# Two loads reordered, the constants' transfer moved behind them, and one test of the first group moved from ScalarE to VectorE

## The chip, the core and the metric

The kernel runs on one core of a Trainium2 chip. A core has five engines that run side by side, each through its own instructions in order: TensorE (PE; its weight loads are PEld), VectorE (DVE), ScalarE (ACT), GpSimd (POOL) and SyncE (SP, which here only issues DMAs; SPq and ACTq are the queues that issue). Transfers run on 16 DMA engines. The metric is the device time of one execution in microseconds, as the median of several runs.

## The reference

A gated linear attention with a complex gate, then a feed-forward block:

```python
mag = np.sqrt(a_re * a_re + a_im * a_im)
scale = np.minimum(mag, 0.999) / (mag + 1e-06)
a_re_n, a_im_n = (a_re * scale, a_im * scale)
for t in range(S):
    new_re = ar * S_re - ai * S_im
    new_im = ar * S_im + ai * S_re
    S_re, S_im = (new_re + kv, new_im)
    y[:, :, t] = einsum('bhd,bhde->bhe', q[:, :, t], S_re)
# x: (B*S, H*D)
h = x @ w_in
solu = h * softmax(h)
ln = (solu - mean) / sqrt(var + 1e-06) * g_ln
return ln @ w_out
```

B = 4, H = 8, S = 768, D = 48; 3072 tokens of width 384 go through a hidden width of 1024. The weights arrive as float64.

## The kernel before

The sequence is cut into six stretches of 128 positions. Two batches of one stretch form a **group** (12 groups, numbered 0 to 11); a tile of a group is 128 positions by 768 columns (2 batches x 8 heads x 48). Each group holds two **chunks**, 24 in all, which go through attention and the feed-forward block one after the other.

For a group, `prep_steps` turns the gate into a logarithm of its size and an angle, so that the recurrence becomes running sums, which TensorE makes by a triangular matrix out of a table of constants `mats`. The steps, with their lines:

- `inverse` (L824, L825, ScalarE): lr = Ln(ar), x0 = Exp(-lr), which is 1/ar.
- `ratio` (L830, L831, VectorE): ai = ai * x0, x0 = ar * x0. The second is 1 up to the error of the inverse.
- `sure` (L834, ScalarE): the test of the inverse. It adds up (x0 - 1) squared over the row into `seen`; a verdict at the end of the kernel compares this with a bound, and a general version follows if it is exceeded.
- `tangent` (L839, VectorE): x0 = (x0 - 2) * ai, a corrected ratio, written over x0.
- `square`, `secant` (L842, L845, ScalarE): ar = x0 squared, u = Ln(ar + 1). `fourth` (L848, ScalarE): ar squared into ai, with its sum into `seen`, another test.
- `size` (L852, VectorE), `eps` (L855, L856, ScalarE), `lnm` (L859, VectorE): the logarithm of the clamped size, in lr.
- `total` (L881, TensorE): running sums of lr; `grow` (L893) and `decay` (L896, ScalarE): their exponentials into ai and ar, with which k and q are scaled (L908, L904, VectorE).
- `angle` (L922, ScalarE): the arctangent of x0, in place; then phases, `nearest` (L938, into the tile f), sine and cosine.

For group 0 alone, the steps from `inverse` to `angle` and the loads of a_re and a_im are done in two halves of 384 columns, a and b. The test `sure` of half b adds up in a slot of its own. For the other groups both halves are one instruction.

The order of the instructions on all engines is written out by hand in the string `ORDER`: a list of step names with the number of their group, chunk or weight piece. Each engine receives its instructions in this order, and waits at each for what it needs. All loads are issued by SP in this order, so a DMA that has to wait keeps those behind it waiting. Ahead of the first step stand a load of ScalarE's table, the DMA of the constants, issued by ScalarE (L1280), and some memsets.

The weights are fetched in seven pieces (`fetch`), of which ScalarE (`raised`, L752) and VectorE (`convert`, L758 to L762) make float32 values in between the first groups. `last` (L900) sends the last row of the decays through a DMA.

Tiles named ar and ai have two buffers each, by turns for the groups; lr, x0 and u have one, f has one.

Of the kernel before, what the change touches and what calls it, by code (L numbers as in the profile page):

```python
# [516 lines left out]
init:0 load_aia:0 load_ara:0 inversea:0 load_arb:0 ratioa:0 load_aib:0 surea:0 load_q:0 tangenta:0 fetch:5 fetch:1  # L517
inverseb:0 squarea:0 ratiob:0 secanta:0 sureb:0 sizea:0 load_v:0 tangentb:0 epsa:0 load_k:0 lnma:0 squareb:0 secantb:0
fourthb:0 sizeb:0 total0:0 epsb:0 fourtha:0 raised:5 lnmb:0 decay0:0 grow0:0 total1:0 grow1:0 decay1:0 fetch:0 trig:0
anglea:0 convert:5 phase0:0 last:0 raised:1 qs0:0 angleb:0 convert:1 phase1:0 nearest0:0 part0:0 turn_ends:0  # L520
nearest1:0 ks0:0 ks1:0 sina:0 cosa:0 load_ai:1 qs1:0 part1:0 q2:0 tot:0 sinb:0 k2:0 cosb:0 exp:0 qt1:0 load_ar:1 qT1:0
raised:0 q2:1 kt1:0 k2:1 convert:0 kT1:0 inverse:1 ratio:1 kt0:0 qt0:0 qT0:0 kT0:0 fetch:2 score1:0 fetch:6 qt0:1
qT0:1 load_vr:0 score0:0 qt1:1 sure:1 raised:2 load_q:1 mask0:0 values:0 tangent:1 kt1:1 fetch:3 square:1 secant:1
turned_x:0 convert:2 qT1:1 up0:0 fetch:4 raised:6 size:1 eps:1 convert:6 lnm:1 fourth:1 onward:0 up1:0 gain:0 total1:1
load_k:1 kT1:1 raised:3 exp0:0 grow1:1 total0:1 decay0:1 grow0:1 carry:1 convert:3 solu0:0 decay1:1 trig:1 angle:1
kt0:1 phase1:1 ks1:1 qs0:1 kT0:1 add:1 phase0:1 ks0:1 score1:1 raised:4 nearest0:1 score0:1 nearest1:1 convert:4
part0:1 carry:0 part1:1 mean:0 mean:3 mean:7 add:0 sin:1 cos:1 mask0:1 load_q:2 q2:2 k2:2 mean:1 zt0:0 exp:1 load_ar:2
mean:4 mean:2 inverse:2 values:1 mean:5 kqb:2 turned_x:1 load_ai:2 ratio:2 mean:6 zT0:0 meansum:0 again:5 last:1
centre:3 centre:7 up1:1 sure:2 tangent:2 load_v:1 kqt0:2 square:2 zt1:0 centre:1 centre:2 secant:2 centre:0 centre:4
size:2 centre:6 eps:2 centre:5 up0:1 k2:3 turn_ends:1 qs1:1 score1:2 lnm:2 onward:1 centred:0 load_vr:1 score0:2 tot:1  # L530
down0:0 total0:2 zT1:0 total1:2 load_k:2 q2:3 exp0:1 fourth:2 mask0:2 down1:0 solu0:1 decay0:2 grow0:2 grow1:2
load_ar:3 decay1:2 kqb:3 trig:2 mixed:1 zt0:1 kqt0:3 last:2 values:2 angle:2 spread:0 zT0:1 on:2 phase1:2 ks1:2 norm:0
qs0:2 turned_x:2 phase0:2 carry:2 load_ai:3 nearest1:2 nearest0:2 up0:2 part1:2 part0:2 sin:2 add:2 cos:2 ks0:2 k2:4
q2:4 centred:1 exp:2 zt1:1 zT1:1 inverse:3 scale:0 up1:2 kqb:4 score1:3 score0:3 down0:1 mask0:3 ratio:3 exp0:2
turn_ends:2 spread:1 sure:3 solu0:2 load_q:3 values:3 tangent:3 load_v:2 down1:1 square:3 tot:2 turned_x:3 secant:3
size:3 load_k:3 carry:3 qs1:2 up0:3 kqt0:4 eps:3 norm:1 up1:3 k2:5 onward:2 zt1:2 lnm:3 lh:3 zt0:2 exp0:3 q2:5 scale:1
zT0:2 zT1:2 fourth:3 score1:4 ll:3 score0:4 mixed:0 total0:3 load_vr:2 total1:3 down0:2 kqb:5 down1:2 solu0:3 decay0:3
grow0:3 grow1:3 decay1:3 mask0:4 add:3 centred:2 trig:3 blocks:3 values:4 angle:3 on:3 xh:3 kqt0:5 store:1 store:0
spread:2 xl:3 last:3 phase1:3 turned_x:4 phase0:3 ks0:3 ks1:3 qs0:3 nearest0:3 score1:5 load_ar:4 centred:3 score0:5
nearest1:3 carry:4 load_ai:4 norm:2 part0:3 up0:4 part1:3 sin:3 cos:3 up1:4 mask0:5 turn_ends:3 exp:3 add:4 scale:2  # L540
k2:6 q2:6 away:3 inverse:4 values:5 exp0:4 kqb:6 ratio:4 down0:3 load_q:4 solu0:4 spread:3 turned_x:5 sure:4 load_v:3
tangent:4 qs1:3 down1:3 carry:5 kqt0:6 square:4 blocks:4 secant:4 size:4 onward:3 up0:5 away:4 eps:4 k2:7 norm:3 up1:5
q2:7 lnm:4 lh:4 tot:3 fourth:4 score1:6 ll:4 score0:6 exp0:5 total0:4 load_vr:3 load_k:4 kqb:7 total1:4 kqt0:7 solu0:5
scale:3 decay0:4 grow0:4 grow1:4 decay1:4 mask0:6 add:5 down0:4 trig:4 down1:4 centred:5 values:6 angle:4 on:4 xh:4
centred:4 qs0:4 xl:4 spread:4 last:4 store:2 phase1:4 turned_x:6 phase0:4 ks1:4 nearest0:4 ks0:4 nearest1:4 blocks:5
score1:7 carry:6 load_ai:5 part0:4 load_ar:5 part1:4 norm:4 score0:7 up0:6 sin:4 add:6 turn_ends:4 cos:4 exp:4 scale:4
away:5 store:3 inverse:5 mask0:7 up1:6 k2:8 q2:8 kqb:8 values:7 spread:5 exp0:6 ratio:5 down0:5 sure:5 load_q:5
solu0:6 turned_x:7 load_v:4 tangent:5 down1:5 square:5 qs1:4 kqt0:8 blocks:6 secant:5 onward:4 carry:7 up0:7 norm:5
size:5 eps:5 q2:9 k2:9 away:6 load_vr:4 lnm:5 up1:7 load_k:5 lh:5 fourth:5 scale:5 exp0:7 score1:8 ll:5 score0:8
total0:5 tot:4 kqb:9 total1:5 down0:6 kqt0:9 solu0:7 grow1:5 decay1:5 mask0:8 decay0:5 grow0:5 trig:5 down1:6 add:7  # L550
centred:7 blocks:7 values:8 angle:5 on:5 inspect:5 xh:5 centred:6 xl:5 spread:6 phase1:5 last:5 qs0:5 store:4
turned_x:8 phase0:5 ks1:5 load_ar:6 nearest1:5 nearest0:5 ks0:5 carry:8 load_ai:6 score0:9 score1:9 part1:5 part0:5
mask0:9 up1:8 sin:5 norm:6 up0:8 cos:5 add:8 turn_ends:5 scale:6 exp:5 inverse:6 store:5 k2:10 q2:10 values:9 kqb:10
ratio:6 exp0:8 solu0:8 away:7 turned_x:9 onward:5 down0:7 load_q:6 sure:6 down1:7 load_v:5 spread:7 tangent:6 square:6
blocks:8 qs1:5 kqt0:10 carry:9 secant:6 fourth:6 up0:9 norm:7 size:6 k2:11 away:8 eps:6 lnm:6 tot:5 load_vr:5 up1:9
q2:11 lh:6 scale:7 exp0:9 load_k:6 score0:10 score1:10 ll:6 total0:6 kqb:11 total1:6 down0:8 kqt0:11 solu0:9 grow1:6
decay1:6 mask0:10 decay0:6 grow0:6 trig:6 down1:8 add:9 centred:9 blocks:9 angle:6 values:10 on:6 xh:6 centred:8
store:6 xl:6 qs0:6 spread:8 last:6 phase1:6 turned_x:10 phase0:6 nearest0:6 ks1:6 nearest1:6 score1:11 carry:10
load_ai:7 score0:11 ks0:6 load_ar:7 away:9 part0:6 part1:6 cos:6 up0:10 sin:6 norm:8 mask0:11 up1:10 turn_ends:6
scale:8 exp:6 add:10 inverse:7 spread:9 store:7 values:11 k2:12 q2:12 kqb:12 ratio:7 exp0:10 down0:9 onward:6 solu0:10  # L560
load_q:7 turned_x:11 sure:7 down1:9 tangent:7 qs1:6 carry:11 load_v:6 kqt0:12 square:7 blocks:10 up0:11 secant:7
size:7 norm:9 eps:7 k2:13 away:10 load_vr:6 scale:9 lnm:7 tot:6 up1:11 q2:13 lh:7 fourth:7 exp0:11 score1:12 load_k:7
ll:7 score0:12 total0:7 kqb:13 total1:7 down0:10 centred:10 kqt0:13 solu0:11 grow1:7 decay1:7 mask0:12 decay0:7
grow0:7 trig:7 down1:10 add:11 blocks:11 angle:7 values:12 on:7 xh:7 last:7 store:8 spread:10 centred:11 qs0:7 xl:7
ks0:7 phase1:7 turned_x:12 phase0:7 nearest1:7 ks1:7 nearest0:7 score0:13 score1:13 part1:7 part0:7 mask0:13 sin:7
load_ar:8 away:11 carry:12 load_ai:8 up0:12 cos:7 add:12 norm:10 turn_ends:7 scale:10 exp:7 store:9 up1:12 k2:14 q2:14
inverse:8 values:13 kqb:14 ratio:8 exp0:12 solu0:12 down0:11 load_q:8 turned_x:13 sure:8 down1:11 load_v:7 tangent:8
carry:13 qs1:7 spread:11 kqt0:14 square:8 blocks:12 secant:8 norm:11 size:8 onward:7 k2:15 tot:7 eps:8 away:12 lnm:8
load_vr:7 fourth:8 up0:13 lh:8 load_k:8 up1:13 q2:15 score1:14 score0:14 ll:8 scale:11 total0:8 kqb:15 total1:8
exp0:13 decay0:8 grow0:8 centred:12 mask0:14 grow1:8 decay1:8 down0:12 kqt0:15 solu0:13 trig:8 down1:12 add:13  # L570
centred:13 blocks:13 angle:8 values:14 on:8 xh:8 store:10 spread:12 xl:8 last:8 phase1:8 turned_x:14 phase0:8 ks0:8
score0:15 qs0:8 nearest0:8 score1:15 ks1:8 nearest1:8 part0:8 carry:14 load_ai:9 part1:8 sin:8 norm:12 mask0:15 cos:8
add:14 load_ar:9 up1:14 turn_ends:8 exp:8 up0:14 away:13 k2:16 q2:16 scale:12 inverse:9 store:11 values:15 kqb:16
ratio:9 exp0:14 spread:13 load_v:8 solu0:14 turned_x:15 sure:9 down0:13 load_q:9 down1:13 tangent:9 blocks:14 square:9
# [38 lines left out]
def whole(ctx, tc, flag, q, k, v, a_re, a_im, moe_w_in, moe_w_out, moe_g_ln, out):  # L613
# [193 lines left out]

    def prep_steps(g):
        ti, b0 = g * GB // B, g * GB % B
        split = g >= 3  # L810

        class Tiles(dict):
            def __missing__(self, nm):
# [27 lines left out]
        def square(cs):  # L841
            nc.scalar.activation(out=st["ar"][:, cs], in_=st["x0"][:, cs], func=AF.Square)  # L842
# [531 lines left out]
```

## Time and profile before

| | us |
|---|---|
| median of 3 runs | 415.65 (415.19 to 415.83) |
| the profiled execution: its time | 415.1 |
| the profiled execution: its span | 413.1 |

| engine | busy us | share of the span |
|---|---|---|
| PE | 379.1 | 92% |
| DVE | 337.0 | 82% |
| ACT | 299.0 | 72% |
| POOL | 64.5 | 16% |

The span lies between the first and the last instruction; the profiled execution's time is 2.0 us longer than its span. The page cuts the span into 40 slices of 10.3 us; a digit is the busy share of a slice in tenths:

```
PE   0368779999999999999999999999999999999995
DVE  3798999779799899899988899889988988855530
ACT  4997977977887777887877976877976967721332
PEclk9999999999999999999999999999999999999998
```

In the first slices TensorE is little used; later on it is full nearly to the end. PEclk is the clock that TensorE was granted. In a row of the order of time, the first number is the start in us from the beginning of the span, the second the duration; then come the engine, the line, the operation, the tile written and the tiles read, and in brackets how long the engine sat idle before and what it waited for.

### The profile page before, as it was taken

To read this page: it belongs to the slowest core of one execution; us is meant where nothing else is said; L and a number is where in the kernel's file an instruction comes from. 1 tells how busy PE (TensorE), PEld (TensorE's weight loads), DVE (VectorE), ACT (ScalarE), POOL (GpSimd) and SP (SyncE) were. 2 spreads that over 40 slices of the span, in tenths; PEclk is the share of its full clock that TensorE was granted. 3 is DMA by queue.
4 is the path that set the end of the run, shared out by engine and by line. 5 is a ranking of instruction groups with operands and counts; after the bars stand their busy time and mean duration, and the time that the engine had idled before them with its cause. 6 is when DMAs were issued, how large, how long until landed. Compare 5 with 4: busy or idle time off the path is not lost.

```text
span 413.1 us, 15874 instructions
## 1 busy us (share of the span) xinstructions
PE 379.1 (92%) x6968; PEld 202.7 (49%) x6968; DVE 337.0 (82%) x414; ACT 299.0 (72%) x487; POOL 64.5 (16%) x140
## 2 busy tenths in 40 slices
PE   0368779999999999999999999999999999999995
PEld 0025334455645554654554554555645656546543
DVE  3798999779799899898899889988988988855530
ACT  4997977977887777887877976877976967721332
POOL 3000000112112112112122112112112122101111
PEclk9999999999999999999999999999999999999998
DMA  9995947695877778877787877967759768797551
GB/s 216 286 280 153 222 101 171 159 211 128 207 165 170 167 177 180 182 157 167 179 175 165 207 163 160 206 157 172 163 138 215 158 155 206 232 208 187 171 216 49
DMA packets 167741, 74.17 MB, mean 180 GB/s; under 512 B 142576, under 2 KB 156016, under 8 KB 166896
## 3 DMA queue, kind: packets, MB, share of 16 engines
q1 hardware_dynamic: 167376, 72.64, 74.7%
q8 instruction: 57, 0.93, 0.9%
q10 hardware_dynamic: 288, 0.43, 0.4%
q14 instruction: 20, 0.16, 0.1%
HBM read 38.87 MB, written 4.72 MB: 106 GB/s over the span
## 4 chain that ended last, share of the span: by engine, by line
PE 81%; ACT 8%; DVE 5%; DMA 2%; issue 1%; SPq 1%; DVEq 0%; ACTq 0%
PE f_h L1128 28%; PE f_o L1193 27%; PE f_y L1087 9%; PE f_score L1054 7%; PE f_d L1095 3%; PE f_L L876 2%; PE f_phase L876 2%; DMA f_q<-in_q_dram 1%; DMA f_ar<-in_a_re_dram 1%; ACT f_cs L951 1%; PE f_y L1203 1%; PE f_o L1203 1%; ACT L986 1%; ACT L989 1%; DVE f_kb L1009 1%
## 5 line engine op out<-in xcount | busy, mean ns | idle before, releaser
L1128 PE MATMUL f_h<-f_w_in,f_xT 128*32 128x512 f32 x1152 | 131.4, 593 | 1.4 <-ACT f_xT L1121 1.2
L1193 PE MATMUL f_o<-f_w_mix,f_zT 128*32 128x384 f32 x1280 | 108.6, 487 | 0.0
L1128 PEld LDWEIGHTS f_h<-f_w_in,f_xT 128*32 128x32 f32 x1152 | 40.9, 110 | 66.4 <-issue 64.3
L1193 PEld LDWEIGHTS f_o<-f_w_mix,f_zT 128*32 128x32 f32 x1280 | 42.8, 110 | 54.1 <-issue 51.5
L1009 DVE STREAM_TRANSPOSE f_kb<-f_kq 128x1536 f32<-128x1536 f32 x22 | 56.5, 2570 | 1.4 <-DMA f_kqT<-f_kb 0.7
L1140 DVE SCALAR_TENSOR_TENSOR f_z<-f_h,f_z 128x1024 f32<-128x1024 f32 x24 | 29.1, 1213 | 13.5 <-ACT f_z L1136 13.5
L1180 POOL TENSOR_SCALAR f_s<-f_s,f_sum 128x1 f32<-128x1 f32 x24 | 11.7, 485 | 182.1 <-ACT f_z L1174 181.9
L1136 ACT ACTIVATE f_z<-f_h 128x1024 f32<-128x1024 f32 x24 | 24.4, 1018 | 21.0 <-PE f_h L1128 21.0
L1087 PE MATMUL f_y<-f_att,f_v 128*16 128x128 f32 (+1 forms) x384 | 36.7, 273 | 0.8 <-DVE f_att L1059 0.8
L1054 PEld LDWEIGHTS f_score<-f_kqT 96*32 96x32 f32 x1536 | 32.5, 112 | 10.0 <-issue 10.0
L1087 PE MATMUL f_y<-f_att,f_vr 128*32 128x128 f32 x384 | 36.8, 273 | 0.0
L1059 DVE TENSOR_TENSOR f_att<-f_score,f_mats 128x1024 f32<-128x1024 f32 x24 | 29.3, 1220 | 8.5 <-PE f_score L1054 8.4
L1054 PE MATMUL f_score<-f_kqT 96*32 96x64 f32 (+3 forms) x1536 | 34.0, 238 | 0.0
L1087 PE MATMUL f_y<-f_kqT,f_state 96*32 96x128 f32 (+1 forms) x640 | 33.2, 272 | 0.0
L1174 ACT ACTIVATE f_z<-f_z,f_less 128x1024 f32<-128x1024 f32 x24 | 27.3, 1138 | 0.0
L869 POOL TENSOR_TENSOR f_ll<-f_lr,f_lh 128x768 fp32r<-128x768 f32 x9 | 16.6, 1849 | 65.6 <-ACT f_lh L864 57.9
L1087 PEld LDWEIGHTS f_y<-f_att,f_v 128*32 128x32 f32 (+1 forms) x384 | 22.0, 103 | 7.5 <-issue 6.4
L1158 DVE STREAM_TRANSPOSE f_zb<-f_z 128x1024 f32<-128x1024 f32 x20 | 24.8, 1238 | 0.0
L1000 DVE TENSOR_TENSOR f_kq<-f_cs,f_k 128x768 f32<-128x768 f32 x24 | 22.9, 955 | 2.1 <-ACT f_cs L951 1.2
L1000 DVE TENSOR_TENSOR f_kq<-f_cs,f_q 128x768 f32<-128x768 f32 x24 | 22.9, 953 | 1.1 <-PE f_d L1095 0.5
L1087 PEld LDWEIGHTS f_y<-f_att,f_vr 128*32 128x32 f32 x384 | 22.3, 109 | 1.7 <-issue 1.7
L1171 POOL TENSOR_SCALAR f_less<-f_sum 128x1 f32<-128x1 f32 x24 | 6.3, 266 | 88.7 <-DVE f_z L1140 88.7
(124 smaller groups left out, 643.9 us busy)
## 6 DMA issues: line engine op xcount, KB each, us to landing
f_kqT<-f_kb SPq DMA_DIRECT2D x88, 192.0 KB, 3.3
f_zT<-f_zb SPq DMA_DIRECT2D x80, 128.0 KB, 3.1
f_raw<-in_moe_w_out_dram SPq DMA_DIRECT2D x14, 384.0 KB, 5.0
f_raw<-in_moe_w_in_dram SPq DMA_DIRECT2D x5, 1024.0 KB, 6.7
f_q<-in_q_dram SPq DMA_DIRECT2D x12, 384.0 KB, 4.9
f_v<-in_v_dram SPq DMA_DIRECT2D x12, 384.0 KB, 5.2
f_k<-in_k_dram SPq DMA_DIRECT2D x12, 384.0 KB, 3.9
out_dram<-f_ot SPq DMA_DIRECT2D x23, 192.0 KB, 3.6
```

Source lines behind the costliest of these rows:

```text
L869: nc.gpsimd.tensor_tensor(out=t, in0=st[src], in1=st[hi].bitcast(FP), op=OP.subtract)
L1000: nc.vector.tensor_tensor(out=t, in0=T["cs", g][:, i * H:(i + 1) * H], in1=heads(T[nm, g][:, i]).unsqueeze(2).to_broadcast([P, H, 2, D]), ...
L1009: nc.vector.transpose(out=t, in_=T["kq", c].rearrange("p n h (f j) -> p j (n h) f", j=3))
L1054: nc.tensor.matmul(out=scores[r0:r0 + 32, x, r:], lhsT=QK[:, r // 32, x], rhs=QK[:, r // 32:, H + x], start=True, stop=True)
L1059: nc.vector.tensor_tensor(out=st["att"].rearrange("p (i u) t -> p i u t", u=2), in0=scores.rearrange("p (i u) t -> p i u t", u=2), in1=mat ...
L1087: nc.tensor.matmul(**product)
L1128: nc.tensor.matmul(out=st["h"][r:r + 32, half * 512:(half + 1) * 512], lhsT=st["xT"][:, c * P + r:c * P + r + 32], rhs=w_in[:, c, half * 5 ...
L1136: nc.scalar.activation(out=z, in_=h, func=AF.Exp, accum_out=sums[:, n:n + 1])
L1140: nc.vector.scalar_tensor_tensor(out=st["z"], in0=st["h"], scalar=1.0, in1=st["z"], op0=OP.mult, op1=OP.mult, accum_out=st["sum"][:, 0:1])
L1158: nc.vector.transpose(out=st["zb"], in_=st["z"].rearrange("p (c s f) -> p s c f", s=4, f=32))
L1174: nc.scalar.activation(out=st["z"], in_=st["z"], func=AF.Square, bias=st["less"], accum_out=st["sum"][:, 1:2])
L1193: nc.tensor.matmul(out=st["o"][rows], lhsT=zT, rhs=w[:, c], start=(c == 0), stop=(c == KF - 1))
```

## The change

It has three parts, all at the start of the kernel; the order behind the first 33 entries of `ORDER` is the same.

- The DMA of the constants leaves its place ahead of all steps on ScalarE's queue and becomes a step of its own on SP's queue, behind the four half loads of a_re and a_im and ahead of q. The first half of a_re is loaded ahead of the first half of a_im.
- For group 0 the test `sure` is done by two VectorE instructions, x0 = x0 - 1 and then x0 * x0 with a sum, in place of one of ScalarE. It stands behind `tangent`.
- So that the test still finds x0, `tangent` of group 0 writes to ai instead; `square` and `angle` read it there, `fourth` writes to f, and `grow` to lr, where the scaling of k reads it.

The order, cut to what differs:

```diff
-init:0 load_aia:0 load_ara:0 inversea:0 load_arb:0 ratioa:0 load_aib:0 surea:0 load_q:0 tangenta:0 fetch:5 fetch:1
-inverseb:0 squarea:0 ratiob:0 secanta:0 sureb:0 sizea:0 load_v:0 tangentb:0 epsa:0 load_k:0 lnma:0 squareb:0 secantb:0
+init:0 load_ara:0 load_aia:0 inversea:0 load_arb:0 ratioa:0 load_aib:0 constants:0 load_q:0 tangenta:0 surea:0 fetch:5
+fetch:1 inverseb:0 squarea:0 ratiob:0 secanta:0 sizea:0 load_v:0 tangentb:0 sureb:0 epsa:0 load_k:0 lnma:0 squareb:0
+secantb:0
...
```

The steps:

```diff
+        tan, up = ("ai", "lr") if g == 0 else ("x0", "ai")
...
         def sure(cs, o=g):
-            nc.scalar.activation(out=st["u"][:, cs], in_=st["x0"][:, cs], func=AF.Square, bias=mone,
-                                 accum_out=seen[:, 1, o:o + 1])
+            x0 = st["x0"][:, cs]
+            if g == 0:
+                nc.vector.tensor_scalar(out=x0, in0=x0, scalar1=-1.0, scalar2=None, op0=OP.add)
+                nc.vector.scalar_tensor_tensor(out=x0, in0=x0, scalar=1.0, in1=x0, op0=OP.mult, op1=OP.mult,
+                                               accum_out=seen[:, 1, o:o + 1])
+            else:
+                nc.scalar.activation(out=st["u"][:, cs], in_=x0, func=AF.Square, bias=mone, accum_out=seen[:, 1, o:o + 1])
 
         def tangent(cs):
             ai, x0 = st["ai"][:, cs], st["x0"][:, cs]
-            nc.vector.scalar_tensor_tensor(out=x0, in0=x0, scalar=2.0, in1=ai, op0=OP.subtract, op1=OP.mult)
+            nc.vector.scalar_tensor_tensor(out=st[tan][:, cs], in0=x0, scalar=2.0, in1=ai, op0=OP.subtract, op1=OP.mult)
 
         def square(cs):
-            nc.scalar.activation(out=st["ar"][:, cs], in_=st["x0"][:, cs], func=AF.Square)
+            nc.scalar.activation(out=st["ar"][:, cs], in_=st[tan][:, cs], func=AF.Square)
...
         def fourth(cs, o=g):
-            nc.scalar.activation(out=st["ai"][:, cs], in_=st["ar"][:, cs], func=AF.Square, accum_out=seen[:, 0, o:o + 1])
+            nc.scalar.activation(out=st["f" if g == 0 else "ai"][:, cs], in_=st["ar"][:, cs], func=AF.Square,
+                                 accum_out=seen[:, 0, o:o + 1])
...
         def grow(i):
-            nc.scalar.activation(out=st["ai"][:, i * DM:(i + 1) * DM], in_=st["L", i], func=AF.Exp, scale=-1.0)
+            nc.scalar.activation(out=st[up][:, i * DM:(i + 1) * DM], in_=st["L", i], func=AF.Exp, scale=-1.0)
...
-            nc.vector.scalar_tensor_tensor(out=x, in0=st["ai"][:, i * DM:(i + 1) * DM], scalar=MOST_K, in1=x, op0=OP.min,
+            nc.vector.scalar_tensor_tensor(out=x, in0=st[up][:, i * DM:(i + 1) * DM], scalar=MOST_K, in1=x, op0=OP.min,
...
         def angle(cs):
-            nc.scalar.activation(out=st["x0"][:, cs], in_=st["x0"][:, cs], func=AF.Arctan)
+            nc.scalar.activation(out=st["x0"][:, cs], in_=st[tan][:, cs], func=AF.Arctan)
```

The constants:

```diff
     to_exp()
-    nc.scalar.dma_start(out=mats, in_=nc.inline_tensor(fast_constants(), name="f_mats_np").ap().rearrange("p (n t) -> p n t", n=5))
...
+    def constants():
+        nc.sync.dma_start(out=mats, in_=nc.inline_tensor(fast_constants(), name="f_mats_np").ap().rearrange("p (n t) -> p n t", n=5))
+
+    steps["gain", 0], steps["constants", 0] = gain, constants
```

## The prediction

> **What bounds the kernel now.** I read the span in slices first, then busy time by stretch, then the order of time in the first 20 us. The answer by stretch has, for each engine, busy microseconds and (instructions):
>
> ```profile
> core 0: us, PE busy (x) PEld busy (x) DVE busy (x) ACT busy (x) POOL busy (x), PEclk, DMA share, GB/s
> 0.00:10.00 10.00, 0.00 (x0) 0.00 (x0) 3.36 (x14) 4.39 (x9) 3.48 (x11) 1.00 0.89 210
> 10.00:20.00 10.00, 3.01 (x16) 0.40 (x16) 7.02 (x13) 9.45 (x20) 0.00 (x0) 1.00 0.99 301
> 20.00:30.00 10.00, 6.25 (x34) 2.51 (x34) 9.32 (x13) 9.21 (x16) 0.00 (x0) 1.00 0.98 273
> ...
> 100.00:200.00 100.00, 99.84 (x1942) 54.30 (x1930) 89.26 (x104) 79.31 (x128) 17.71 (x36) 1.00 0.77 172
> ```
>
> From about 60 us on TensorE is full (99.84 of 100 us) at a granted clock of 1.00, so nothing in the change touches its rate; but it can't fill until the first group has been prepared. From 10 to 60 us ScalarE and VectorE run at 9 of 10 us and hand work to each other. The change acts ahead of that. What it can do is start the dense stretch earlier; then everything behind moves as a block. The order of time shows the head (start, duration, engine, line, idle before):
>
> ```profile
> 0.72 0.45 SPq L706 DMA_DIRECT2D f_ai<-in_a_im_dram  x1
> 0.75 0.39 ACTq L1280 DMA_DIRECT2D f_mats<-f_mats_np  x1
> ...
> 1.23 2.38 SPq L706 DMA_DIRECT2D f_ar<-in_a_re_dram  x2
> ...
> 5.58 0.52 ACT L824 ACTIVATE f_lr<-f_ar 128x384 f32<-128x384 f32 x1 [3.58 <-DMA f_ar<-in_a_re_dram]
> 6.13 0.52 ACT L825 ACTIVATE f_x<-f_lr 128x384 f32<-128x384 f32 x1
> 6.69 0.56 DVE L830 TENSOR_TENSOR f_ai<-f_ai,f_x 128x384 f32<-128x384 f32 x1 [4.34 <-ACT f_x L825]
> 7.28 0.56 DVE L831 TENSOR_TENSOR f_x<-f_ar,f_x 128x384 f32<-128x384 f32 x1
> ...
> 7.87 0.61 ACT L834 ACTIVATE f_u<-f_x,f_bias 128x384 f32<-128x384 f32 x1 [1.22 <-DVE f_x L831]
> ...
> 8.39 0.19 ACT L834 ACTIVATION_READ_ACCUMULATOR f_u<-f_x,f_bias 128x1 f32 x1
> 8.49 0.51 ACT L824 ACTIVATE f_lr<-f_ar 128x384 f32<-128x384 f32 x1
> 8.61 0.56 DVE L839 SCALAR_TENSOR_TENSOR f_x<-f_x,f_ai 128x384 f32<-128x384 f32 x1 [0.78 <-ACT f_u L834]
> ...
> 15.61 0.56 DVE L859 SCALAR_TENSOR_TENSOR f_lr<-f_lr,f_u 128x384 f32<-128x384 f32 x1 [1.33 <-ACT f_u L856]
> ```
>
> The first computation waits 3.58 us for a_re, which is issued behind a_im. Then the test (L834) holds up two things: the tangent (L839), which overwrites what it reads, and the second half's inverse (8.49), queued behind it on ScalarE although its a_re landed at 6.46. The last line, lnm of the second half at 15.61, opens the dense stretch. Its new start is the number to find.
>
> **a_re first, constants behind.** Landings before, from issue plus time to landing: a_im first half 4.6, a_re first half 5.56, a_re second 6.46, a_im second 7.36. The DMA answers in 0.2 us windows, by queue (packets, MB, share of 16 engines), from 2.6 and from 3.4 us:
>
> ```profile
> q10 hardware_dynamic: 25, 0.06, 79.7%
> q1 hardware_dynamic: 13, 0.00, 6.0%
> ...
> q1 hardware_dynamic: 272, 0.05, 127.5%
> ```
>
> q10 is the constants, q1 the loads. The loads' first packet comes at about 2.62, 1.90 after issue, and until 3.1 they go packet for packet against the far larger ones of the constants. Then 272 per 0.2 us: a half's 1024 packets take 0.75 us. Counting them up, the first load's last packet is at 3.84; it landed 0.78 later.
>
> Now a_re is issued at 0.72 with nothing beside it. Latest: it lands when the first load did, 4.62. Middle: same first packet, full rate at once, 2.65 + 0.75 + 0.78 = 4.18. Nearest row: a_im of the second group, same 192-byte runs, issued at 20.00 into idle engines, starts at 21.22 and, with its ramp, has 1024 packets through 2.19 after issue; that gives 0.72 + 2.19 + 0.78 = 3.69. The constants' own first packet came 0.95 after issue, as a weight fetch's at 38.79 did, so nothing points to a slow start-up. I take 3.85, close to that row, keeping a third of the gap to the middle case. Gain at the first Ln: 5.58 - 3.85 = **1.73** (bounds 0.96 to 1.89). a_im's first half follows at about 4.7, the next halves at 5.55 and 6.4, by 0.75 to 0.85 each.
>
> Here the Trainium skill speaks against the move: "DMA: Bandwidth & Descriptors", Rules for kernel authors, says that queues of different engines share the same 16 DMA engines and interleave, so that the issuing queue only decides who pays the issue time. By that alone the constants' move saves nothing and costs SP 0.39; the swap of order alone would stay: 0.96. But the packet counts show that interleaving is what delays the first load. I go by them.
>
> **What the queues pay.** SP issues the constants (0.39) ahead of q, fetch 5, fetch 1, v, k and fetch 0. The constants' packets take 1.13 us of 16 engines (q10's shares summed); about 0.4 of that fell where loads can now run, so everything behind them lands some 0.7 later. Cover, with users 2.1 earlier (below): fetch 5 lands 11.6, now 12.3, first used (ScalarE, L752) at 15.99, now 13.9; q 9.2, used at 18.65; fetch 1 15.06, used by VectorE at 19.12; k 18.1, used at 23.22; fetch 0 20.9, used at 28.51. The tightest has 1.2 us left. Constants: behind four halves, last packet about 6.6, landed 7.5; the first matmul wants them at about 11.2. SP is free of fetch 0 at about 17.0 and its next step, the end rows, is ready at 16.6: 0.4 late, against 1.5 of slack before TensorE reads them at 23.48. No cost.
>
> **The test on VectorE.** Per half ScalarE loses L834 with its read of the accumulator, 0.71 on the path. VectorE gains a subtraction and an accumulating product behind the tangent. Subtraction: L758 took 552 ns for 768 and 686 for 1024 columns, so about 0.35 for 384 (0.56 if it ran like a TENSOR_TENSOR). Product: 0.55 like L852; its accumulator read is 0.08 at L1140 and overlaps. With gaps 0.03, 0.96 a half: more than on ScalarE, but nothing needs its result. The trace has no accumulating product of two SBUF operands (L1140 reads PSUM). For it the skill's "Vector Engine (DVE) Microarchitecture Reference", section 7, states half throughput with two non-bf16 SBUF sources, as none is left to read the accumulator. L852 without accumulation ran 384 columns in 0.55; halved, some 0.95. I take 0.55, the nearest row; the rule's 0.40 more lies on the path once.
>
> **The sum, in order of time.** ScalarE inverse a 3.85 to 4.92 (two of 0.52). VectorE ratio a 4.96 to 6.11, tangent a to 6.70, test a to 7.66. ScalarE meanwhile does inverse b from 5.55 to 6.62 (before: 8.49), then square a 6.73, secant a to 7.87. VectorE ratio b follows the test, 7.65 to 8.80, then size a 8.72 to 9.27. Here ScalarE waits: VectorE has become the later one. Eps a 9.29 to 10.54; tangent b (9.19) and test b (to 10.71) lie under that, lnm a 10.63. ScalarE square b 10.44, secant b to 11.59, fourth b to 12.10; size b 11.62 to 12.17; eps b 12.19 to 13.45; lnm b at **13.48** instead of 15.61: 2.13 earlier, 1.73 from the landing and 0.40 from the test. ScalarE's 1.42 us of tests do not become 1.42 us of gain, since test a now stands in front of ratio b and size a.
>
> **Edits at nothing.** Tangent, grow and fourth go to other tiles. fourth's tile f is next written by nearest on the same engine; grow's lr is read last by the k scaling at 24.2 and next written by the second group's inverse at 30.03: 5.8 us of cover, without which that Ln would wait. The second group's a_im has its own buffer.
>
> **Behind lnm b.** ScalarE and VectorE are back to back to 60 us, and their feeds have slack. The odd-head values land at about 33.9 for a product at 36.05; the DMA idle time at 20.3 to 21.3 closes up, so they move about 0.8 and have 0.9 left, and ScalarE picks that product up only at 38.61. So I carry 2.1 whole to the end: span 413.1 to 411.0, that run 415.1 to 413.0; from the median of 415.65, **413.55**.
>
> **Rivals.**
> First, my forecast, 60%: 413.55, own range 413.2 to 414.3 (first landing at 3.69, or at 4.62).
> Second, the dearer test: half throughput and a slow subtraction, 0.40 + 0.21 on the path: gain 1.5, 414.15. For it: the skill's statement and no near row. Against: L852. 12%.
> Third, the transfers hold the head back. The DMA share is 0.98 from 10 to 30 us, and the bulk gets later, not earlier. If a fetch of 20 to 35 us binds, only the closed-up idle time of 0.8 is won: 414.85. Against: the slacks above. 16%.
> Fourth, slower: SP stalls on the constants. One load there (k) took 6.24 us to issue[...]. If the fifth issue met that, fetch 5 would land at 11.6 + 6.2 = 17.8 instead of in time for 15.99, and ScalarE holds decay and grow behind it: 1.8 slower, 417.45. It decides from a stall of 4.4 us on. Against: only some 0.4 MB stands ahead of the constants, and the second half of a_re met the same with 1.77. 8%.
> Fifth, no effect: the gain is eaten by a wait between ScalarE and VectorE in the 40 us after: 415.65, 4%.
>
> **Chances.** 0.2% is 0.83 us, about what can be told from no change. Faster: all of the first and second and half of the third, 0.80; within: 0.11; slower: 0.09. The range goes down to 412.9 (0.65 for a start of packets sooner than the idle row) and up to 415.0, past the third case.
>
> **What would show it.** The first Ln at 3.7 to 4.2; inverse b right behind inverse a; test a 0.9 long on VectorE with ScalarE idle some 1.4 us ahead of eps a; lnm b near 13.5; L752 unchanged against its neighbours; the same offset at 60 us and at the end. A first Ln at 4.6, a product of 0.95 us, or an offset that shrinks between 15 and 60 us would prove me wrong.

## The result, and the profile after

| | before, us | after, us | ratio of after to before, 95% interval |
|---|---|---|---|
| first comparison, medians of 9 and 9 | 415.65 | 413.31 | 0.993 (0.9912 to 0.9947) |
| second, of 18 and 8 | 415.83 | 413.23 | 0.9932 (0.9908 to 0.9955) |
| third, of 17 and 5 | 415.64 | 413.08 | 0.9932 (0.9914 to 0.9949) |

The changed kernel is faster, by 2.3 to 2.6 us in the medians and by 2.8 to 2.9 us by the ratios. Applied to 415.65, the first ratio gives 412.7, just under the lower end of the predicted range (412.9); the median of 413.31 lies inside it. Forecast was 413.55, a gain of 2.1 us. So the direction is as predicted and the gain is 0.2 to 0.8 us more than forecast, and it has to be asked where that comes from.

Below, the **head** is the stretch up to lnm of half b, the step that opens the dense stretch. The order of time there in the changed kernel, first of three profiles (start, duration, engine, line, idle before):

```profile
0.72 0.45 SPq L707 DMA_DIRECT2D f_ar<-in_a_re_dram  x1
...
3.48 0.87 SPq L1311 DMA_DIRECT2D f_mats<-f_mats_np  x1
3.55 0.52 ACT L826 ACTIVATE f_lr<-f_ar 128x384 f32<-128x384 f32 x1 [1.55 <-DMA f_ar<-in_a_re_dram]
...
4.66 0.56 DVE L832 TENSOR_TENSOR f_ai<-f_ai,f_x 128x384 f32<-128x384 f32 x1 [2.31 <-ACT f_x L827]
...
5.38 0.52 ACT L826 ACTIVATE f_lr<-f_ar 128x384 f32<-128x384 f32 x1 [0.75 <-DMA f_ar<-in_a_re_dram]
5.85 0.56 DVE L846 SCALAR_TENSOR_TENSOR f_ai<-f_x,f_ai 128x384 f32<-128x384 f32 x1
...
6.44 0.36 DVE L838 TENSOR_SCALAR f_x<-f_x 128x384 f32<-128x384 f32 x1
6.83 0.56 DVE L839 SCALAR_TENSOR_TENSOR f_x<-f_x 128x384 f32<-128x384 f32 x1
...
7.32 0.08 DVE L839 DVE_READ_ACCUMULATOR f_x<-f_x 128x1 f32 x1
7.32 0.55 DVE L832 TENSOR_TENSOR f_ai<-f_ai,f_x 128x384 f32<-128x384 f32 x1
...
8.97 0.61 ACT L863 ACTIVATE f_u<-f_lr,f_bias 128x384 f32<-128x384 f32 x1 [1.36 <-DVE f_lr L860]
...
13.21 0.56 DVE L867 SCALAR_TENSOR_TENSOR f_lr<-f_lr,f_u 128x384 f32<-128x384 f32 x1 [1.33 <-ACT f_u L864]
```

The first Ln waits 1.55 us for its data where it waited 3.58. The Ln of half b is at 5.38 instead of 8.49. The two instructions of the test (L838, L839) stand between the tangent at 5.85 and the ratio of half b at 7.32; eps of half a waits 1.36 us for VectorE. lnm of half b is at 13.21: 2.40 us earlier than before.

The DMA answer in 0.2 us windows, for 1.8 and for 2.6 us (packets, MB, share of 16 engines):

```profile
q1 hardware_dynamic: 79, 0.02, 43.5%
...
q1 hardware_dynamic: 267, 0.05, 123.5%
```

From 2.6 us the loads move 267 packets in 0.2 us, where they had 13 beside the constants. Their first packets come in the window from 1.8 us, 1.1 to 1.3 after issue instead of 1.9.

Busy time by stretch, the columns as before:

```profile
core 0: us, PE busy (x) PEld busy (x) DVE busy (x) ACT busy (x) POOL busy (x), PEclk, DMA share, GB/s
0.00:10.00 10.00, 0.00 (x0) 0.00 (x0) 6.36 (x22) 5.50 (x9) 3.48 (x11) 1.00 0.89 207
10.00:20.00 10.00, 4.86 (x28) 0.80 (x32) 7.48 (x12) 9.47 (x19) 0.00 (x0) 1.00 0.95 283
20.00:30.00 10.00, 6.38 (x62) 3.59 (x54) 9.72 (x14) 9.32 (x17) 0.00 (x0) 0.75 1.08 308
...
100.00:200.00 100.00, 100.00 (x2014) 54.92 (x2010) 88.88 (x105) 79.16 (x128) 18.71 (x37) 1.00 0.79 176
```

VectorE's first 10 us hold 3.0 us more work than before: the tests, and what has moved up. The dense part is unchanged. The granted clock in this execution fell to 0.75 between 20 and 30 us.

To follow the gain through the span, I took the start of each chunk's copy of the attention output (ScalarE, L1121 before and L1129 after) and subtracted its start in the one profile of the kernel before. Three profiles of the changed kernel, in us:

| at the copy of chunk (time before) | first | second | third |
|---|---|---|---|
| 0 (38.61) | -2.51 | -1.98 | -2.19 |
| 1 (58.51) | -2.50 | -1.20 | -2.18 |
| 6 (138.84) | -2.51 | -1.20 | -2.19 |
| 8 (169.30) | -2.77 | -0.92 | -2.55 |
| 18 (320.20) | -2.60 | -1.10 | -2.21 |
| 19 (330.38) | -2.62 | -0.23 | -1.37 |
| last scaling (408.00) | -2.89 | -0.51 | -1.01 |

The gain is there at 38 us in all three. From there on it stays the same to 0.1 us over long stretches, and jumps at few places, by up to 0.9 us, differently in each execution of the same code. Some of the jumps belong to the one execution of the kernel before that all are measured against: at chunk 8, nine of the twelve other profiles on record, of whatever kernel, gain 0.3 to 0.4 us.

### The profile page after: what moved, and what is told of

Its sections match the earlier page's. It is cut to its first block, busy times and chain, and to the rows that moved or that the text cites. A ratio compares the mean times of both kernels' runs of the same rounds, so it can differ in the third digit from the quotient of the medians.

```text
span 410.0 us, 15879 instructions
## 1 busy us (share of the span) xinstructions
PE 378.6 (92%) x6968; PEld 201.6 (49%) x6968; DVE 338.3 (83%) x420; ACT 298.0 (73%) x483; POOL 64.7 (16%) x140
## 4 chain that ended last, share of the span: by engine, by line
PE 84%; ACT 9%; DVE 4%; issue 2%; DMA 1%; ACTq 0%; DVEq 0%
PE f_h L1136 29%; PE f_o L1201 27%; PE f_y L1095 9%; PE f_score L1062 7%; PE f_d L1103 3%; PE f_L L884 2%; PE f_phase L884 2%; ACT f_bits L753 1%; PE f_phase L889 1%; ACT L994 1%; DMA f_ar<-in_a_re_dram 1%; PE f_y L1211 1%; PE f_o L1211 1%; ACT L997 1%; DVE f_w_in L763 1%
## 5 line engine op out<-in xcount | busy, mean ns | idle before, releaser
L1228 ACT ACTIVATE f_ot<-f_o,f_rs 128x384 f32<-128x384 f32 x23 | 13.1, 571 | 9.6 <-PE f_o L1201 5.1
```

## The experiments

The parts one by one, each against the kernel before as it ran beside it (416.43 us beside the first four, 415.83 and 415.64 beside the later ones). A time in a profile is that of one execution. `...` marks what is left out of a diff.

**The order of the loads alone.**

```diff
-init:0 load_aia:0 load_ara:0 inversea:0
+init:0 load_ara:0 load_aia:0 inversea:0
```

> The kernel before with one edit: the first half of a_re is loaded ahead of the first half of a_im; the constants stay on ScalarE's queue, ahead of all. Theory (the constants' packets delay the first load, and order is worth one slot): a_re lands in the slot that a_im had, so the first Ln starts at 4.6 us instead of 5.58 and lnm of half b at 14.65 instead of 15.61; about 1.0 us gained. Rival (the order alone did it, the constants cost the loads nothing): first Ln at 3.55 as in the changed kernel, lnm b at 13.6, 2.0 us gained.

Measured: 415.17 against 416.43, ratio 0.9974 (0.9960 to 0.9988). The order of time of this kernel:

```profile
0.75 0.39 ACTq L1280 DMA_DIRECT2D f_mats<-f_mats_np  x1
4.66 0.52 ACT L824 ACTIVATE f_lr<-f_ar 128x384 f32<-128x384 f32 x1 [2.66 <-DMA f_ar<-in_a_re_dram]
...
14.69 0.56 DVE L859 SCALAR_TENSOR_TENSOR f_lr<-f_lr,f_u 128x384 f32<-128x384 f32 x1 [1.33 <-ACT f_u L856]
```

4.66 was what the slot of the first load promised, and lnm b was at 14.69. The rival's 3.55 is out: the order alone is worth one slot, 0.92 us.

**The constants behind the loads alone.** a_im's half stays first.

```diff
-    nc.scalar.dma_start(out=mats, ...)
...
+    def constants():
+        nc.sync.dma_start(out=mats, ...)
...
-load_arb:0 ratioa:0 load_aib:0 surea:0
+load_arb:0 ratioa:0 load_aib:0 constants:0 surea:0
```

> The kernel before with one edit: the constants are issued by SP behind the four half loads; a_im's first half is still ahead of a_re's. Theory: the loads' first packet comes at 1.85 us instead of 2.62; a_re's first half lands where the second load of the changed kernel did, 4.43, so first Ln at 4.45 and lnm b at 14.5; about 1.1 us gained. Rival (the queue only decides who pays the issue time): first Ln stays at 5.5, nothing gained.

Measured: 415.60 against 416.43, ratio 0.9979 (0.9962 to 0.9996). The order of time of this kernel:

```profile
4.45 0.52 ACT L824 ACTIVATE f_lr<-f_ar 128x384 f32<-128x384 f32 x1 [2.44 <-DMA f_ar<-in_a_re_dram]
...
14.48 0.56 DVE L859 SCALAR_TENSOR_TENSOR f_lr<-f_lr,f_u 128x384 f32<-128x384 f32 x1 [1.33 <-ACT f_u L856]
```

First Ln at 4.45, lnm b at 14.48: 1.13 us each, with the order of a_im and a_re as before. The constants did hold the loads up.

**Both edits of the loads, the test as before.** The two diffs above together.

> The kernel before with both edits of the loads (a_re's half first, constants behind on SP), the test still on ScalarE ahead of the tangent. Theory: first Ln at 3.55, and the rest of the preparation as long as before (10.03 us from first Ln to lnm b), so lnm b at 13.58; 2.0 us gained, and the test's move is worth the other 0.37 of the changed kernel. Rival (ScalarE's 1.42 us of tests are what counts): the changed kernel stays more than 1 us ahead of this one.

Measured: 414.42 against 416.43, ratio 0.9961 (0.9942 to 0.9979). The order of time of this kernel:

```profile
3.66 0.52 ACT L824 ACTIVATE f_lr<-f_ar 128x384 f32<-128x384 f32 x1 [1.66 <-DMA f_ar<-in_a_re_dram]
...
5.04 0.56 DVE L830 TENSOR_TENSOR f_ai<-f_ai,f_x 128x384 f32<-128x384 f32 x1 [2.70 <-DMA f_ai<-in_a_im_dram]
...
13.96 0.56 DVE L859 SCALAR_TENSOR_TENSOR f_lr<-f_lr,f_u 128x384 f32<-128x384 f32 x1 [1.33 <-ACT f_u L856]
```

From the first Ln on it took 10.30 us instead of 10.03: the ratio of half a waited for a_im's half, until 5.04. The three profiles of the changed kernel have lnm b at 13.21, 13.55 and 13.34, so 0.4 to 0.75 ahead. The rival asked for over 1 us, and in the head it is out. By the ratios to the kernel before, the changed kernel is 1.2 us ahead of this one, but the intervals overlap and the two did not run beside each other, so the time alone does not rule the rival out.

**The test on VectorE alone**, with the tiles that go with it; loads and constants as before.

```diff
-load_aib:0 surea:0 load_q:0 tangenta:0
+load_aib:0 load_q:0 tangenta:0 surea:0
...
-secanta:0 sureb:0 sizea:0 load_v:0 tangentb:0 epsa:0
+secanta:0 sizea:0 load_v:0 tangentb:0 sureb:0 epsa:0
...
```

> The kernel before with the test of group 0 on VectorE behind the tangent and the other tiles that go with it; loads and constants as before. Theory: first Ln at 5.58, from there to lnm b 9.66 us as in the changed kernel, so lnm b at 15.24; 0.37 us gained, too little to tell by the time alone. Rival: the 1.42 us that ScalarE is rid of come back whole, lnm b at 14.2.

Measured: 415.88 against 416.43, ratio 0.999 (0.9975 to 1.0005), not to be told from no change. The order of time of this kernel:

```profile
5.58 0.52 ACT L826 ACTIVATE f_lr<-f_ar 128x384 f32<-128x384 f32 x1 [3.57 <-DMA f_ar<-in_a_re_dram]
...
6.56 0.51 ACT L826 ACTIVATE f_lr<-f_ar 128x384 f32<-128x384 f32 x1
...
8.86 0.56 DVE L839 SCALAR_TENSOR_TENSOR f_x<-f_x 128x384 f32<-128x384 f32 x1
...
9.35 0.55 DVE L832 TENSOR_TENSOR f_ai<-f_ai,f_x 128x384 f32<-128x384 f32 x1
...
10.99 0.61 ACT L863 ACTIVATE f_u<-f_lr,f_bias 128x384 f32<-128x384 f32 x1 [1.36 <-DVE f_lr L860]
...
15.24 0.56 DVE L867 SCALAR_TENSOR_TENSOR f_lr<-f_lr,f_u 128x384 f32<-128x384 f32 x1 [1.33 <-ACT f_u L864]
```

The Ln of half b starts at 6.56 instead of 8.49, 1.93 us earlier. But the ratio of half b, behind the test on VectorE, starts at 9.35, where it started at 9.58 before. Almost all of ScalarE's lead is waited away, and lnm b is at 15.24: 0.37 us.

The sum of the parts at lnm b is 0.92 + 1.13 + 0.37 = 2.42 us, and the changed kernel has 2.40, 2.06 and 2.27 (both edits of the loads together had 1.65, less than their 2.05 apart, for a_im's half came in between). So the changed kernel has nothing in the head beyond its parts.

**The constants twice.** To see whether the delay goes with the size of the constants' transfer, the kernel before loads them a second time, into a tile used only later.

```diff
     nc.scalar.dma_start(out=mats, ...)
+    spare = zbp.tile([P, FF], FP, tag="zb", name="f_spare")
+    nc.scalar.dma_start(out=spare[:, 0:5 * P], ...)
```

> The kernel before with the constants' transfer doubled: the same 320 KB once more, on ScalarE's queue right behind the first, into a tile that is not used until later. Theory (the loads wait for the constants' packets): the loads' first packets stay few until both copies are through, some 1.0 us later than before; first Ln at about 6.6, lnm b at 16.6, 1.0 us lost. Rival (the loads' late first packet in the kernel before is a start-up of SP's queue, the constants only share a little): first Ln at 5.6 to 5.9.

Measured: 418.07 against 415.64, ratio 1.005 (1.0032 to 1.0069). The order of time of this kernel:

```profile
6.54 0.52 ACT L824 ACTIVATE f_lr<-f_ar 128x384 f32<-128x384 f32 x1 [4.53 <-DMA f_ar<-in_a_re_dram]
...
16.56 0.56 DVE L859 SCALAR_TENSOR_TENSOR f_lr<-f_lr,f_u 128x384 f32<-128x384 f32 x1 [1.33 <-ACT f_u L856]
```

6.54 instead of 5.58, and lnm b at 16.56: 0.95 us later for 320 KB more, where 320 KB less at that time made it 1.13 us earlier. A start-up time of SP's queue would not have grown. In detail I was wrong: the loads' packets stayed few only to about 3.2 us, then flowed, and went down again from 68 to 5 per 0.2 us between 4.0 and 4.4 while the second copy came through. The time rose by 2.1 us by the ratio, more than the head's 0.95; the rest comes behind the head and was not followed.

**The constants behind the loads, but from ScalarE's queue.**

```diff
     def constants():
-        nc.sync.dma_start(out=mats, ...)
+        nc.scalar.dma_start(out=mats, ...)
```

> The changed kernel with the constants issued by ScalarE again, but behind inverse a instead of ahead of everything. Theory (time, not queue, decides): first Ln at 3.55 as in the changed kernel, lnm b at 13.2, total within 0.2% of it; the constants start their transfer at about 5 us and land well before the first matmul at 10.9. Rival (it is SP's queue behind the loads that matters): the loads of b's halves get slower and lnm b is later by 0.5 us or more.

Measured: 413.88 against 415.83, ratio 0.9941 (0.9921 to 0.9962); the changed kernel beside it 0.9932 (0.9908 to 0.9955). First Ln at 3.41, the earliest of all; lnm b at 13.71, later by 0.16 than the 13.55 of the changed kernel beside it, and by 0.50 than its first profile. So most of the gain does not hang on the queue: it is the time of issue that decides for the first load. Whether the queue has a small part in the halves of b, of 0.2 us or so, one profile that lies just outside the changed kernel's own spread (13.21 to 13.55) can't tell.

**The tests further back.** In the changed kernel test a stands on VectorE ahead of the ratio of half b. Here it stands behind the tangent of half b, and test b behind size b.

```diff
-load_q:0 tangenta:0 surea:0 fetch:5
+load_q:0 tangenta:0 fetch:5
...
-tangentb:0 sureb:0 epsa:0
+tangentb:0 surea:0 epsa:0
...
-sizeb:0 total0:0
+sizeb:0 sureb:0 total0:0
```

> The changed kernel with the two tests further back in the order: test a behind tangent b, test b behind size b. Theory (in the changed kernel test a stands on VectorE in front of ratio b and size a, and ScalarE waits 1.36 us for size a): ratio b starts at 6.5 instead of 7.32, ScalarE's wait shrinks to about 0.6, lnm b at 12.46 instead of 13.21; 0.75 us gained over the changed kernel, if the feeds of the head (fetch 1, the end rows) are still early enough. Rival (VectorE's order there costs nothing, the wait is for secant a): lnm b stays at 13.2.

> The changed kernel with test a behind tangent b and test b behind size b, again. Its profile had lnm b 0.5 and 0.9 us ahead of two profiles of the changed kernel. Theory (the head passes through to the end): 0.5 to 0.8 us, about 0.2%, ahead of the changed kernel in the medians of all runs of both. Rival (something behind the head takes it back): no difference, as in the first medians nearly (0.39 us).

**The test left out**, in group 0 alone.

```diff
             if g == 0:
-                nc.vector.tensor_scalar(out=x0, in0=x0, scalar1=-1.0, ...)
-                nc.vector.scalar_tensor_tensor(out=x0, in0=x0, scalar=1.0, in1=x0, ..., accum_out=seen[:, 1, o:o + 1])
+                pass
```

> The changed kernel without the test of the inverse in group 0 (left out; its sum stays zero, all else is computed). Theory: without it ratio b and size a move up as in the kernel with the tests further back, lnm b at 12.46; no more than that is to be had from the test, in whatever place. Rival (the test costs more than its place): clearly ahead of the kernel with the tests further back.

**The changed kernel again**, beside these.

> The changed kernel once more, beside the three that follow, to have its time and profile on the same chip. If the head alone is what moved, its gain over the kernel before is 2.4 to 2.6 us at 60 us and the same at the end; if the last 0.3 to 0.4 us that its first profile won behind 340 us belong to the change, they are there again.

> The changed kernel a third time, beside the one with the tests further back, to tell the two apart by more runs. Expected again 0.993 to 0.994 of the kernel before; first Ln at 3.5, lnm b at 13.2 to 13.6.

| | lnm b, us | median, us | ratio to before, interval |
|---|---|---|---|
| changed kernel, second | 13.55 | 413.23 | 0.9932 (0.9908 to 0.9955) |
| changed kernel, third | 13.34 | 413.08 | 0.9932 (0.9914 to 0.9949) |
| tests further back | 12.68 | 412.84 | 0.9928 (0.9905 to 0.9952) |
| tests further back, again | 12.93 | 413.64 | 0.9938 (0.9917 to 0.9959) |
| no test | 12.50 | 413.44 | 0.9936 (0.9912 to 0.9960) |

The order of time with the tests further back, first profile:

```profile
6.79 0.56 DVE L832 TENSOR_TENSOR f_ai<-f_ai,f_x 128x384 f32<-128x384 f32 x1 [0.41 <-DMA f_ai<-in_a_im_dram]
...
8.44 0.61 ACT L863 ACTIVATE f_u<-f_lr,f_bias 128x384 f32<-128x384 f32 x1 [0.86 <-DVE f_lr L860]
...
8.79 0.35 DVE L838 TENSOR_SCALAR f_x<-f_x 128x384 f32<-128x384 f32 x1
...
12.68 0.56 DVE L867 SCALAR_TENSOR_TENSOR f_lr<-f_lr,f_u 128x384 f32<-128x384 f32 x1 [0.46 <-ACT f_u L864]
```

The head does what the theory says: the ratio of half b no longer stands behind the test (in this profile it waits for its a_im, the wait that has taken its place), and lnm b comes 0.9 and 0.4 us earlier than in the changed kernel beside it, near the kernel with no test at all. But the time does not follow: the two comparisons have 412.84 and 413.64, the changed kernel 413.31, 413.23 and 413.08. The 0.5 to 0.8 us expected of the second comparison did not come. No difference can be told, and I can't call this version better; nor is the kernel with no test ahead of it (413.44), as its rival wanted.

What was expected of the changed kernel's second profile did not come either: its offset at 58 us was 1.20 us instead of 2.4 to 2.6, and 0.51 at the end, so what the first profile won behind 340 us can't be put down to the change.

One profile shows how such a gain gets lost. Stretches of the second profile with the tests further back:

```profile
core 0: us, PE busy (x) PEld busy (x) DVE busy (x) ACT busy (x) POOL busy (x), PEclk, DMA share, GB/s
...
55.00:60.00 5.00, 3.21 (x18) 1.02 (x22) 4.92 (x6) 2.77 (x6) 0.00 (x0) 0.82 0.37 77
60.00:65.00 5.00, 5.00 (x40) 1.31 (x32) 5.00 (x9) 3.22 (x4) 0.00 (x0) 0.84 0.67 159
```

At the copies of chunks 0 and 1 it was 3.10 us ahead of the kernel before; at chunk 2 it was 1.41 ahead. Between them the granted clock was 0.82 and 0.84 for 5 us each: 5 x 0.18 + 5 x 0.16 = 1.7 us of full clock, as much as is missing. The kernel with no test lost the same 1.7 us at the same place, with 0.83 and 0.82. In the second profile of the changed kernel the clock was 0.77 and 0.89 from 45 to 55 us, again 1.7 us of full clock; there the offset shrank by only 0.8 us (1.98 to 1.20 in the table above). The first profile of the changed kernel had its low clock elsewhere:

```profile
core 0: us, PE busy (x) PEld busy (x) DVE busy (x) ACT busy (x) POOL busy (x), PEclk, DMA share, GB/s
25.00:30.00 5.00, 4.05 (x44) 2.74 (x42) 4.83 (x6) 4.96 (x8) 0.00 (x0) 0.50 1.03 347
30.00:35.00 5.00, 4.20 (x79) 3.25 (x75) 4.19 (x6) 3.46 (x6) 0.00 (x0) 0.81 1.00 235
```

Clocks of 0.50 and 0.81 there cost nothing: lnm b was 2.40 ahead and chunk 0's copy 2.51. TensorE was busy for 4.05 and 4.20 of 5 us even so, which means that it still waited for other engines. The third profile of the changed kernel had no low stretch (mean clock 0.999) and kept 2.19 and 2.18 from 38 to 58 us. What sets the place of these stretches was not tried.

## Why the prediction was right in kind, and which steps failed in size

The forecast was a gain of 2.1 us, and by the ratios 2.8 to 2.9 came. Two steps failed in their size. The term for the first Ln was put at 1.73 us and measured 1.9 to 2.1, of which 0.1 us on average came through to the end of the head. And the step that carried the head's gain whole to the end put the difference from one execution to the next behind the head at nothing. Most of the miss stands there: by the ratios 0.6 us on average, and its cause stays open.

**What bounds.** Right. Every part that moved lnm b moved the copy of chunk 0 with it (2.40 and 2.51 in the first profile, 2.06 and 1.98 in the second, 2.27 and 2.19 in the third; 0.92 and 0.84 with the order of the loads alone, 1.13 and 1.05 with the constants alone).

**a_re first, constants behind.** Right in kind, too small in size. I put the first Ln at 3.85, for 1.73 us. The three profiles of the changed kernel have 3.55, 3.50 and 3.68, for 1.9 to 2.1, all ahead of the 3.7 to 4.2 that I had named as the sign. The step that failed is the choice inside it: from the nearest row (3.69, a load into idle engines) I went back by a third of the way to the middle case, in case the late first packet of before was a start-up of the queue. With the constants away the first packets came 1.1 to 1.3 us after issue, as in that row (1.22), and doubling the constants moved the first Ln by another 0.96. There was no start-up to allow for. (The constants' own first packet, put at 0.95 after issue, came at 1.03; the argument stands.) Of the split, the constants are the larger half: 1.13 us, the order 0.92.

The rule that all queues share the same engines, and that the issuing queue only decides who pays the issue time (the Trainium skill, "DMA: Bandwidth & Descriptors", Rules for kernel authors), was weighed against the packet counts. Both hold, for different questions: issued late from either queue, the constants gave nearly the same head (13.71 against 13.55); but issued early, they cost the loads 1.13 us.

**What the queues pay.** Right: nothing in the head waited for the later bulk. Fetch 5's bits were made at 13.59 straight behind their neighbours, and the end rows, late as reckoned, made TensorE wait 0.6 us where nobody waited for it. The rivals of transfers that hold the head back, and of a stalled SP, are out: SP took 0.87 to 1.24 us to issue the constants in the three profiles, far from 4.4.

**The test on VectorE.** Right: 0.36 us for the subtraction (reckoned 0.35) and 0.56 for the product (0.55). The half throughput that the Trainium skill states for two non-bf16 SBUF operands, for want of a port for the accumulator ("Vector Engine (DVE) Microarchitecture Reference", section 7) does not show here, with one float32 tile as both operands: the measurement decides, and it is that of the product without accumulation. So the rival of the dearer test is out. The move was put at 0.40 and alone gave 0.37. VectorE became the later one, with ScalarE idle for 1.36 us ahead of eps a (reckoned 1.4).

**The sum.** lnm b was put at 13.48; the three profiles have 13.21, 13.55 and 13.34, a mean of 13.37. So the earlier first Ln did not come through whole. The sum had a_im's first half at about 4.7, in time for a ratio at 4.96; with an earlier first Ln that ratio is ready earlier, and a_im can become the later one. So it was in the second profile:

```profile
3.50 0.52 ACT L826 ACTIVATE f_lr<-f_ar 128x384 f32<-128x384 f32 x1 [1.50 <-DMA f_ar<-in_a_re_dram]
...
5.00 0.56 DVE L832 TENSOR_TENSOR f_ai<-f_ai,f_x 128x384 f32<-128x384 f32 x1 [2.66 <-DMA f_ai<-in_a_im_dram]
```

In the first profile the same ratio ran at 4.66, straight behind the inverse. The 0.34 us between them is the whole difference of the two at lnm b.

**Behind lnm b, and the range.** The gain did pass whole to 60 us in the first and third profiles. In the second the offset shrank from 1.98 us at 38 to 1.20 at 58, which I had named as a sign of being wrong; the granted clock was 0.77 and 0.89 there. Nor was the offset the same at 60 us and at the end: it changed by 0.4, 0.7 and 1.2 us. I had carried 2.1 to the end as if an execution behind the head were the same each time, and had left 0.65 us of room below the forecast. Executions of one kernel differ by 2 us and more (411.93 to 414.07 in the first nine), from the places of low clock and from jumps further back, and the ratio's own interval is 0.7 to 1.0 us to either side. In the medians the gain is 2.3 to 2.6, and by the ratios 2.8 to 2.9. The head accounts for 2.0 to 2.5 of it. The rest, up to 0.9 us, no run settles: it is of the size of what one execution differs from the next behind the head, and the three ratios have the head's 2.2 us (0.9947) at or just inside the upper end of their intervals. Across the parts and variants that gained, the time by the ratio is off the head's gain in both directions, from 0.45 us less (no test) to 0.55 more (the constants from ScalarE's queue), so a real gain behind the head is not shown. The lower edge of the forecast's own range was also mis-summed: a first landing at 3.69 is worth 0.16 us, which makes 413.4 and not 413.2.

**Left open.** Between the copies of chunks 18 and 19 (320 to 330 us) the offset against the kernel before moved by -0.02, +0.87 and +0.84 us in the three profiles of the changed kernel and by +0.82 in that with the order of the loads alone, at a full clock. The traces show where: TensorE's weight loads pause in the middle of a run of them, with nothing that the profile shows to wait for ("issue"). The second profile of the changed kernel, and below the dots a line of its DMA answer from 321.9 to 323.1 us (queue and kind, packets, MB, share):

```profile
323.37 0.12 PEld L1136 LDWEIGHTS f_h<-f_w_in,f_xT 128*32 128x32 f32 x3 [0.31 <-issue]
324.35 0.16 PEld L1136 LDWEIGHTS f_h<-f_w_in,f_xT 128*32 128x32 f32 x8 [0.86 <-issue]
...
q8 instruction: 1, 0.02, 5.4%
```

Gaps of 0.3 us are usual there; this one is 0.86. Behind 70 us the thirteen profiles have 21 such pauses of 0.47 to 1.09 us in the feed-forward block, at varying places, and in every one TensorE goes on 1.3 to 1.6 us after the end of a packet of the queue that the profile calls "instruction" (such packets come every 6 us or so). At 322 us that packet started 0.6 to 1.5 us ahead of the run of weight loads in the three profiles that do not jump there, and up to 0.4 us behind its start in the eight with the largest jumps (0.5 to 0.9 us). That points to instructions that arrive late, but no run changed how they are fetched, so it is a lead and not shown.

## What to carry to other kernels

Count the packets of the first microseconds by queue: a transfer that nobody needs for 10 us, issued beside the load that everybody waits for, cost that load about 1 us here, though it came from another queue. A check that feeds nothing should stand behind the work that feeds something, on whichever engine it runs: moved to another engine but left in front of the next consumer, it gained 0.37 us of the 1.42 it had cost the first. And a gain of half a microsecond at the front of a kernel that is full behind is read in the profile's head, not in the time, when executions differ by 2 us.

## What the runs showed of the hardware

The granted clock fell for some us in the first 65 us (0.50 to 0.98 in windows of 5 us), at 25 to 35, at 45 to 55 or at 55 to 65 us, at two of these, or not at all. A fall that takes 1.7 us of full clock cost 1.7 us at 55 to 65 us and 0.8 us at 45 to 55; one of 3.4 us cost nothing at 25 to 35 us, where TensorE still had idle time. A load's landing scatters too: the first half of a_re, issued at 0.72 us with no constants beside it in eight profiles of five kernels, was used first at 3.41 to 3.68.
